# A Fourier-mixing and cosine-gated MLP kernel: rows ahead of constants in the opening, other fillers for TensorE, weight sums on the engines, one transfer per turned row

## The chip, the cores and the metric

One core of one Trainium2 chip. The metric is device time in microseconds (us). A median of several executions is given with its lowest and highest value. The engines are called as in the profile: PE (TensorE), PEld (its weight loads), DVE (VectorE), ACT (ScalarE), POOL (GpSimd) and SP (SyncE, which only issues transfers here).

## The reference

```python
# x: [8, 3008, 256], w_in: [256, 2048], w_out: [2048, 256], all float32
X = np.fft.fft(x, axis=1)
X = np.fft.fft(X, axis=2)
h = X.real.reshape(8 * 3008, 256) @ w_in
g = h * np.cos(h)
out = g @ w_out
```

## The kernel before

The kernel is already tuned. It has an opening of about 37 us, then 376 equal steps that keep PE busy to the end.

*Opening.* The rows of `x` are loaded in four tiles, half of them by row loads and half, in reversed order, by gathers on POOL. DVE adds and subtracts them ("folds" of rows) into even tiles `e` and odd tiles `o`, and halves these once more. PE applies the sequence transform, and DVE and ACT spread the result into rings: `Rr` (real part), `Ir` (imaginary part), `Rb` (channel 128). Meanwhile the channel transform is multiplied into `w_in`, a quarter at a time ("weight folds"), giving `Wc` for the real and `Ws` for the imaginary part:

```python
def fold_sin(q, tag="H"):                  # fold_cos: the same into Wc
    ps = fold_mms(q, 128, tag)
    act(Ws[:, q * 512 : (q + 1) * 512], ps)

def turn_last(q):                          # row 127 of Ws turned into a column
    for f in range(4):
        c = q * 512 + f * 128
        pin(nc.gpsimd.dma_start(out=wex[q][:, f : f + 1], in_=Ws[127:128, c : c + 128]))
```

*A step.* ACT fills a PSUM bank with channel 128's share, and both matmul groups of the step accumulate on it. So the first of them cannot start before this ACT operation is done. Quarter `q` of `wex` serves steps `2q` and `2q + 1` of eight.

```python
def ext(i):
    S = steps[i] = Step()
    S.H = bank("H")
    for j in range(2):
        f = 2 * (i % 8) + j
        act(S.H[:, j * TW : (j + 1) * TW], Rb[:, cols(i)], scale=wex[f // 4][:, f % 4 : f % 4 + 1])

def mm_P(i):
    first_mm(i, Wc, Rr, 128)      # the real product
def mm_Q(i):
    first_mm(i, Ws, Ir, 127)      # the imaginary product
```

After the cosine gate come seven block products with `w_out`, built from sums of blocks of `G` (by POOL, `sum_1` to `sum_4`) and sums of blocks of the weights, `WT`. The latter are made once:

```python
def add_block(k, r, c):                    # 384 KB, added by the transfer itself
    pin(nc.gpsimd.dma_start(
        out=WT[k][:, 2:8], in_=wout[r][:, 2:8, c * 128 : c * 128 + 128], accum_op=ALU.add))

def less_block(k):                         # a negation on ACT
    v = w2.rearrange("p (i r c) -> p i r c", r=2, c=ND)
    act(WT[k][:, 2:8], WT[2][:, 2:8] if k else v[:, 2:8, 0, 0:128], scale=-1.0)
```

*Order of the opening* (`...` marks cuts):

```python
for _ in range(8):                         # one-row matmuls
    mm(bank("M"), zero[:, 0:128], zero[:, 0:1].to_broadcast([1, 512]), True)
sin(halfpi2)
...
fold_sin(0); turn_last(0); fold_cos(0)
warm(10)                                   # ten more of the same
...
fold_now("c0 e0 o0 c3 e3 o3 c2 e2 o2")
add_O(2, 3)
...
halve_now(0, VE[1])
fold_sin(1); turn_last(1)
first_R.early("pA", "pB")
first_R.copy_e()
...
fold_cos(1)
fold_now("o1 O0 I0")
...
halve_now(1, VO[1])
```

Everything that follows is scheduled by a list of pairs of time and operation, in which `T` is the length of a step and `t = 0` the first real product.

Of the kernel before, what the change touches and what calls it, by code (L numbers as in the profile page):

```python
# [118 lines left out]
def kernel(  # L119
# [47 lines left out]
    xflat = x.rearrange("b s d -> (b s) d")  # L167
    ix = cpool.tile([NP, 9], U32, tag="ix")
    nc.sync.dma_start(out=ix, in_=IX_dr.ap())
    L = [cpool.tile([128, NS * ND], FP, tag=f"xl{j}", name=f"xl{j}") for j in range(4)]  # L170

    def gather_x(b, j, a, z, n):

        pin(
            nc.gpsimd.indirect_dma_start(
                out=L[j][0:NP, a * ND : z * ND],
                out_offset=None,
                in_=xflat,
                in_offset=bass.IndirectOffsetOnAxis(ap=ix[:, n : n + 1], axis=0),
                element_offset=b * SEQ * ND,  # L180
            )
        )
# [26 lines left out]
    for g in gathers(0, ORDER):  # L209
        gather_x(*g)  # L210

    CC = cpool.tile([128, 512], FP, tag="CC")
    w1, MC = [], []
# [6 lines left out]
    wout = moe_w_out.rearrange("(i r p) c -> r p i c", r=2, p=128)  # L220
# [24 lines left out]
    load_mats(0)  # L245
    load_w1(1)
    load_mats(1)
    load_w1(2)
    load_w2(0, 4)
    spin(out=WT[2][:, 2:8], in_=wout[0][:, 2:8, 128:256])  # L250
    load_w2(4, NF)
# [18 lines left out]
    nc.gpsimd.memset(R4, 0.0)  # L270
    nc.gpsimd.memset(Rx4, 0.0)
    zero = cpool.tile([1, 264], BF, tag="zero")
    nc.gpsimd.memset(zero, 0.0)
# [46 lines left out]
    def fold_sin(q, tag="H"):  # L320
        ps = fold_mms(q, 128, tag)
        act(Ws[:, q * 512 : (q + 1) * 512], ps)

    def turn_last(q):

        for f in range(4):
            c = q * 512 + f * 128
            pin(nc.gpsimd.dma_start(out=wex[q][:, f : f + 1], in_=Ws[127:128, c : c + 128]))

    def fold_cos(q, tag="H"):  # L330
        ps = fold_mms(q, 0, tag)
        act(Wc[:, q * 512 : (q + 1) * 512], ps)


    def sum_weights(i, k):
# [4 lines left out]
        gtt(  # L340
# [7 lines left out]

    def add_block(k, r, c):

        pin(
            nc.gpsimd.dma_start(
                out=WT[k][:, 2:8], in_=wout[r][:, 2:8, c * 128 : c * 128 + 128], accum_op=ALU.add
            )
        )

    def less_block(k):

        v = w2.rearrange("p (i r c) -> p i r c", r=2, c=ND)
        act(WT[k][:, 2:8], WT[2][:, 2:8] if k else v[:, 2:8, 0, 0:128], scale=-1.0)  # L360
# [17 lines left out]
    def fold_ops():  # L378
# [20 lines left out]
        for key, V, o, a, b, op in (  # L399
            ("E0", VE, 0, 0, 1, ADD),  # L400
            ("E2", VE, 2, 2, 3, ADD),
            ("R0", VE, 1, 0, 2, ADD),
            ("R1", VE, 3, 0, 2, SUB),
            ("O0", VO, 0, 0, 1, ADD),
            ("I0", VO, 1, 0, 2, SUB),
# [67 lines left out]
    def fold_first():  # L473
# [5 lines left out]
        vtt(a, c[0], c[1], ADD)  # L479
        vtt(g, c[2], c[3], ADD)  # L480
        vtt(a, a, g, ADD)
        z = g[:, 0:4]
        run_now(halve(a, z, 0))
# [52 lines left out]
    class Dft:  # L536
# [18 lines left out]

        def copy_e(self):
# [38 lines left out]

        def minus_sum(self):
# [5 lines left out]
            if self.ri == 0:  # L602
                outs.append((R4[:, self.b : self.b + 1], slice(0, 1)))
# [37 lines left out]
    def load_ext():  # L641
        x1 = spool.tile([128, HALF + 1], FP, tag="rx", bufs=1, name="x1")
        rows = [x1[0 : 2 * NB], x1[2 * NB : 4 * NB]]
        state["rows"] = x1[0 : 4 * NB]

# [420 lines left out]
    for _ in range(8):  # L1066
        mm(bank("M"), zero[:, 0:128], zero[:, 0:1].to_broadcast([1, 512]), True)
    sin(halfpi2)
    def warm(n):

        w = bank("M")
        for _ in range(n):
            mm(w, zero[:, 0:128], zero[:, 0:1].to_broadcast([1, 512]), True)

    fold_sin(0)
    turn_last(0)
    fold_cos(0)
    warm(10)
# [15 lines left out]
    first_R, first_I = Dft(0, 0, 0, held(0, (E[1], Z[0]))), Dft(1, 0, 0)  # L1094

    fold_now("c0 e0 o0 c3 e3 o3 c2 e2 o2")
    add_O(2, 3)
    fold_now("E2")
    pin(nc.vector.tensor_copy(out=L[1][0:1, 7 * ND :], in_=L[0][0:1, 0:ND]))
    fold_now("c1 e1 E0 R0")  # L1100
    halve_now(0, VE[1])
    fold_sin(1)
    turn_last(1)
    first_R.early("pA", "pB")
    first_R.copy_e()
    first_x = Dft(0, 0, 0, fold_first(), Rb, True)
    first_x.early("pC", "pD")
    first_x.copy_e()
    fold_cos(1)
    fold_now("o1 O0 I0")  # L1110
    add_O(2, 0)
    first_R.plus()
    first_x.plus()
    halve_now(1, VO[1])
# [74 lines left out]
    def dve_room(n):  # L1189

        step, late = divmod(n, 2)
        if step < 9:
            return 0.64
# [75 lines left out]
    def plan_dft(b, ri, kodd, n):  # L1269

        d = Dft(ri, b, kodd)
# [20 lines left out]
    for t, fn in (  # L1292
        (0.88, lambda: first_I.early("pA", "M")),
        (0.89, first_I.copy_e),
        (0.95, lambda: fold_sin(2, "pC")),
        (0.96, lambda: turn_last(2)),
        (1.0, first_I.plus),
        (2.9, lambda: fold_cos(2, "pA")),
        (T + 0.95, lambda: fold_sin(3, "pC")),
        (T + 2.9, lambda: fold_cos(3, "pA")),  # L1300
        (3 * T, lambda: turn_last(3)),
        (-0.3, lambda: add_block(2, 1, 1)),
        (1.3, lambda: less_block(0)),
        (1.31, lambda: add_block(0, 0, 1)),
        (T + 0.2, lambda: less_block(1)),
        (T + 0.25, lambda: add_block(1, 0, 0)),
    ):
        at(t, fn)
    for k in range(4):
        at(0.1, lambda k=k: sum_weights(0, k))  # L1310
# [3 lines left out]
    p = pool_all(0, FOLD["R1"])  # L1314
    for i in (1, 2, 3):
# [155 lines left out]
```

## Time and profile before

| | before |
|---|---|
| time at the outset, 3 runs | 1939.3 us (1935.9 to 1940.06) |
| span of the profiled execution | 1936.3 us |
| first real product / first imaginary product | 36.90 / 45.84 us |
| first matmul of step 2 / step 4 / step 8 / step 20 | 55.38 / 67.91 / 90.35 / 161.07 us |
| PE idle, first product to 84 us / 84 to 165 / 165 to 1900 | 5.74 / 5.19 / 3.09 us |
| PE at half clock | until 21.3, and 38.3 to 45.1 us |

A step costs 4.75 us of PE and there is nearly no idle time from 165 us on. So the start of step 8 is the best single number of this case: what the opening has won or lost by then should simply be carried to the end. The prediction shows the lines of the profile.

### The profile page before, as it was taken

How to read it: one execution, taken by the hardware profiler on the slowest of the kernel's cores; microseconds unless marked ns; L12 is line 12 of the kernel's file. 1: busy time of each engine (PE TensorE's matmuls, PEld its weight loads, DVE VectorE, ACT ScalarE, POOL GpSimd, SP SyncE). 2: the span in 40 equal slices, each digit the busy share in tenths (PEclk: the TensorE clock that was granted, in tenths of full speed). 3: DMA queues.
4: the chain of work that ended last, by engine and by line, in shares of the span. 5: the costliest groups of instructions: out<-in, count | busy, mean ns of one | idle time of the engine just before them, and what ended most of it. 6: DMA issues, size and time to landing. Idle time of an engine off the chain costs nothing.

```text
span 1936.3 us, 28827 instructions
## 1 busy us (share of the span) xinstructions
PE 1899.4 (98%) x8951; PEld 1646.7 (85%) x8951; DVE 1450.9 (75%) x2366; ACT 1513.3 (78%) x2985; POOL 1525.5 (79%) x2054
## 2 busy tenths in 40 slices
PE   6899999999999999999999999999999999999998
PEld 3778888888888888888888888888888888888887
DVE  5788877777777777777777777777777777777777
ACT  2767888787878887888788887888878887877886
POOL 4879888898888888888889898888878676655654
PEclk9999999999999999999999999999999999999999
DMA  9724211322123112311231113311212110100101
GB/s 216 51 53 85 50 37 24 72 36 51 29 36 69 35 37 49 52 39 32 45 70 29 45 22 61 52 40 30 31 30 36 20 18 17 20 12 12 23 9 25
DMA packets 263490, 82.16 MB, mean 42 GB/s; under 512 B 240841, under 2 KB 246776, under 8 KB 263336
## 3 DMA queue, kind: packets, MB, share of 16 engines
q1 hardware_dynamic: 249240, 49.04, 14.7%
q0 software_dynamic: 11920, 31.01, 9.3%
q8 instruction: 71, 1.16, 0.3%
q14 instruction: 83, 0.68, 0.1%
q10 hardware_dynamic: 2176, 0.26, 0.1%
HBM read 38.29 MB, written 24.69 MB: 33 GB/s over the span
## 4 chain that ended last, share of the span: by engine, by line
PE 87%; ACT 5%; DVE 5%; issue 1%; POOL 1%; DMA 0%; DVEq 0%; POOLq 0%; ACTq 0%
PE H L292 34%; PE pC L292 15%; PE pD L292 15%; PE pB L292 15%; PE pA L292 8%; ACT G L304 1%; DVE G L829 1%; DVE G L298 1%; ACT M L304 1%; ACT E L304 1%; ACT z L304 1%; POOL G L301 1%; ACT H L304 0%; DVE v L298 0%; DVE M L298 0%
## 5 line engine op out<-in xcount | busy, mean ns | idle before, releaser
L301 POOL TENSOR_TENSOR G<-G 128x256 f32<-128x256 f32 x1500 | 1083.7, 734 | 349.7 <-DVE G L829 281.2
L829 DVE SCALAR_TENSOR_TENSOR G<-H,G 128x512 f32<-128x512 f32 x376 | 259.0, 689 | 225.8 <-ACT G L304 223.5
L298 DVE TENSOR_TENSOR G<-H,G 128x512 f32<-128x512 f32 x376 | 259.7, 691 | 216.5 <-ACT G L304 213.3
L292 PE MATMUL H<-Ir,Ws 127*128 127x256 f32 x1504 | 387.8, 379 | 3.8 <-ACT E L304 3.8
L292 PE MATMUL H<-Rr,Wc 128*128 128x256 f32 x1504 | 388.3, 380 | 2.8 <-ACT H L304 2.7
L292 PE MATMUL pC<-G,WT 128*128 128x256 f32 x1504 | 387.0, 379 | 0.7 <-DVE u L298 0.7
L304 ACT ACTIVATE H<-Rb,wex 128x256 f32<-128x256 f32 x752 | 360.0, 479 | 21.9 <-DVE G L829 9.6
L304 ACT ACTIVATE G<-H 128x512 int32<-128x512 f32 x376 | 223.7, 595 | 177.2 <-DVE G L298 177.2
L304 ACT ACTIVATE E<-H 128x512 f32<-128x512 f32 x376 | 223.7, 595 | 167.7 <-PE H L292 166.3
L292 PEld LDWEIGHTS H<-Ir,Ws 127*128 127x128 f32 x1504 | 283.5, 189 | 48.8 <-ACT E L304 8.5
L292 PEld LDWEIGHTS pC<-G,WT 128*128 128x128 f32 x1504 | 284.1, 189 | 43.2 <-PE H L292 1.5
L292 PEld LDWEIGHTS H<-Rr,Wc 128*128 128x128 f32 x1504 | 281.2, 190 | 43.6 <-ACT H L304 5.6
L304 ACT ACTIVATE G<-G,halfpi 128x512 f32<-128x512 f32 x376 | 269.2, 716 | 3.2 <-DVE G L298 3.0
L298 DVE TENSOR_TENSOR G<-E,H 128x512 f32<-128x512 f32 x376 | 255.1, 679 | 4.4 <-ACT Ws L304 2.5
L298 DVE TENSOR_TENSOR M<-G,M 128x512 f32<-128x512 f32 x376 | 257.5, 685 | 0.0
L829 DVE SCALAR_TENSOR_TENSOR G<-G,M 128x512 f32<-128x512 f32 x376 | 254.3, 676 | 0.5 <-ACT M L304 0.5
L304 ACT ACTIVATE M<-M,halfpi 128x512 f32<-128x512 f32 x376 | 245.2, 652 | 0.0
L292 PE MATMUL pB<-G,WT 128*128 128x256 f32 x752 | 225.4, 381 | 4.7 <-POOL G L301 4.7
L304 ACT ACTIVATE M<-G 128x512 int32<-128x512 f32 x376 | 224.1, 596 | 0.0
L292 PE MATMUL pD<-G,w 128*128 128x256 f32 x752 | 223.8, 379 | 0.1
L292 PE MATMUL pA<-G,w 128*128 128x256 f32 x752 | 223.8, 379 | 0.0
L292 PE MATMUL pB<-G,w 128*128 128x256 f32 x752 | 223.7, 379 | 0.0
(157 smaller groups left out, 2054.6 us busy)
## 6 DMA issues: line engine op xcount, KB each, us to landing
out_dram<-ot SPq DMA_DIRECT2D x496, 32.0 KB
xl<-in_x_dram SPq DMA_DIRECT2D x64, 192.0 KB
o<-o POOLq DMA_DIRECT2D x23, 381.0 KB, 4.9
e<-e POOLq DMA_DIRECT2D x21, 384.0 KB, 5.1
out_dram<-ot SPq DMA_DIRECT2D x256, 2.0 KB
Rb<-r SPq DMA_DIRECT2D x10, 376.0 KB
w<-in_moe_w_in_dram SPq DMA_DIRECT2D x4, 512.0 KB
out_dram<-ot SPq DMA_DIRECT2D x64, 28.0 KB
```

The lines of the kernel that those rows point to most:

```text
L292: nc.tensor.matmul(out_, lhsT=lhsT, rhs=rhs, start=start, stop=stop, skip_group_check=True)
L298: pin(nc.vector.tensor_tensor(out=o, in0=a, in1=b, op=op))
L301: pin(nc.gpsimd.tensor_tensor(out=o, in0=a, in1=b, op=op))
L304: pin(nc.scalar.activation(out=o, in_=i, func=func, **kw))
L829: nc.vector.scalar_tensor_tensor(out=o, in0=h, scalar=TWO_PI, in1=c, op0=ALU.mult, op1=ALU.mult)
```

## The change

Its intent is to have the loop begin sooner and with fewer waits, in five parts.

1. *Rows first.* The constants queue behind the rows on SP. A memset of one element of `CC`, which POOL reaches only after its gathers, holds the constants back.
2. *TensorE's fillers.* 60 and then 6 matmuls on 128 rows of ones take the place of 8 and 10 matmuls on one row, to keep the clock up.
3. *Weight sums on engines.* No accumulating transfers and no negations: POOL sums three of the four pairs of blocks, DVE the fourth.
4. *Channel 128's column.* ACT copies the last row of a quarter in another order, and one transfer turns it, in place of four.
5. *Order.* DVE does the real part whole before it begins the imaginary one, small operations leave it for ACT and POOL, and the weight folds of quarters 1 to 3 all stand behind the first real product.

The diff, cut to its core:

```diff
+    ones = spool.tile([128, 512], FP, tag="v", bufs=1, name="ones").bitcast(BF)
+    pin(nc.vector.memset(ones, 1.0))
...
     for g in gathers(0, ORDER):
-        gather_x(*g)
+        gather_x(*g, table=None if g[1] else first_ix)
     CC = cpool.tile([128, 512], FP, tag="CC")
+    pin(nc.gpsimd.memset(CC[0:1, 0:1], 0.0))
...
+    def take_last(q):
+        t = spool.tile([128, 512], FP, tag=("u", "p3")[q % 2], bufs=1, name="wl")
+        act(
+            t[96:128].rearrange("a (p f) -> a f p", f=4),
+            Ws[96:128, q * 512 : (q + 1) * 512].rearrange("a (f p) -> a f p", f=4),
+        )
+        turned[q] = t
     def turn_last(q):
-        for f in range(4):
-            c = q * 512 + f * 128
-            pin(nc.gpsimd.dma_start(out=wex[q][:, f : f + 1], in_=Ws[127:128, c : c + 128]))
+            pin(nc.gpsimd.dma_start(out=wex[q], in_=turned[q][127:128, :]))
...
-    def add_block(k, r, c): ...
-    def less_block(k): ...
...
         for _ in range(n):
-            mm(w, zero[:, 0:128], zero[:, 0:1].to_broadcast([1, 512]), True)
+            mm(w, ones[:, 0:128], ones[:, 128:640], True)
+    warm(60)
...
-    fold_now("c0 e0 o0 c3 e3 o3 c2 e2 o2")
...
+    fold_now("e0 o0 e3 o3 e2 E2 S0 e1 R0")
+    halve_now(0, VE[3])
...
+    warm(6)
+    fold_now("o2 O2 o1 O0 J0")
     add_O(2, 0)
-    halve_now(1, VO[1])
+    halve_now(1, VO[3])
+    first_R.plus_copy()
...
-        (0.96, lambda: turn_last(2)),
...
+        (0.5, lambda: fold_mm(1, 1)),
+        (0.95, lambda: fold_copy(1, 1)),
+        (0.955, lambda: take_last(1)),
+        (0.96, lambda: turn_last(1)),
...
     for k in range(4):
-        at(0.1, lambda k=k: sum_weights(0, k))
+        at(-0.1, lambda k=k: sum_weights(0, k))
     at(-1.5 * T, load_ext)
...
+    for k in range(4):
+        at(0.98, lambda k=k: sum_weights(1, k))
+        on_pool(1, 0.73, lambda k=k: sum_weights(2, k))
```

`load_ext`, which is not itself changed but for one memset, loads channel 128 of `x` as a row, one float of 4 bytes at a time.

## The prediction

> **What bounds the kernel now.** I read the busy shares of the whole page first, then stretches by time, then the opening instruction by instruction.
>
> ```profile
> PE 1899.4 (98%) x8951; PEld 1646.7 (85%) x8951; DVE 1450.9 (75%) x2366; ACT 1513.3 (78%) x2985; POOL 1525.5 (79%) x2054
> PE 87%; ACT 5%; DVE 5%; issue 1%; POOL 1%; DMA 0%; DVEq 0%; POOLq 0%; ACTq 0%
> ```
>
> The first line is the busy line, the second the chain that ended last. TensorE (PE) sets the time. The next table is the stretches view (stretch, its length, busy time of PE, PEld, DVE, ACT, POOL, granted clock, DMA share, GB/s):
>
> ```profile
> 0.00:10.00 10.00, 4.66 (x8) 0.72 (x8) 0.09 (x2) 1.58 (x2) 6.54 (x17) 1.00 0.80 205
> 10.00:20.00 10.00, 1.73 (x2) 0.84 (x3) 6.38 (x9) 0.00 (x0) 1.84 (x2) 1.00 1.04 273
> ...
> 34.90:38.30 3.40, 1.56 (x6) 0.68 (x4) 3.30 (x4) 1.44 (x3) 3.32 (x4) 1.00 1.57 95
> 38.30:45.20 6.90, 6.43 (x19) 5.39 (x20) 1.37 (x3) 0.97 (x2) 1.63 (x3) 0.51 1.95 95
> 45.20:60.00 14.80, 11.17 (x36) 6.33 (x35) 8.83 (x15) 11.63 (x22) 12.74 (x14) 1.00 1.90 37
> ...
> 165.00:1900.00 1735.00, 1731.91 (x8214) 1517.27 (x8213) 1302.89 (x2126) 1402.24 (x2773) 1393.02 (x1871) 1.00 0.20 37
> ```
>
> From 165 us on PE idles 3 of 1735 us, so nothing but the opening can give time here. In the opening PE waits, and from 38.3 to 45.2 us it works at half clock (0.51). The timeline shows what it waits for:
>
> ```profile
> 11.76 1.21 DVE L373 TENSOR_TENSOR e<-xl 96x1016 f32<-96x1016 f32 x1
> ...
> 26.79 1.60 DVE L373 TENSOR_TENSOR e<-e 96x512 f32<-96x512 f32 x3
> ...
> 33.78 0.54 DVE L298 TENSOR_TENSOR Rr<-ab,pB 128x377 f32<-128x377 f32 x1
> ...
> 35.40 3.26 DVE L373 TENSOR_TENSOR o<-o 96x508 f32<-96x508 f32 x3
> ...
> 36.90 1.13 PE L292 MATMUL H<-Rr,Wc 128*128 128x256 f32 x4 [1.57 <-ACT H L304]
> 38.77 1.14 PE L292 MATMUL pA<-MC,o 95*128 95x95 f32 x4 [0.74 <-issue]
> ...
> 43.11 2.90 PE L292 MATMUL pC<-w,CC 128*128 128x512 f32 x4
> ...
> 45.84 1.03 PE L292 MATMUL H<-Ir,Ws 127*128 127x256 f32 x4
> ...
> 59.47 0.70 PE L292 MATMUL pB<-G,WT 128*128 128x256 f32 x2 [2.11 <-POOL G L301]
> ...
> 71.08 0.70 PE L292 MATMUL pB<-G,WT 128*128 128x256 f32 x2 [1.28 <-POOL G L301]
> ```
>
> The real-part fold runs on DVE from 11.7 to 28.4 us, the imaginary one to 38.7. The main loop's first matmul starts at 36.90; its second half (the Ir product) only at 45.84, behind the transform and a weight fold at half clock. Later PE waits for POOL's block sums (2.11 and 1.28 us). The PE gaps between 36.9 and 84 us add up to 5.7 us.
>
> **What the Trainium skill says.** (1) "TensorE: Matmul & The Clock Gate", Part 1: the clock is halved by default and after an idle window of about 3.4 us, and freed after a busy window of that length. The trace agrees: the stretch 34.9 to 38.3 has PE busy only 1.56 us of 3.4, and the next 6.9 us run at 0.51. It also shows what the page does not say: eight matmuls of one row, busy 4.66 us in the first 10, did not free the clock, because the weight loads of the first fold are 0.85 us apart at 19.25, 20.11 and 20.96 and 0.43 apart from 21.54 on. (2) "DMA: Bandwidth & Descriptors", "Issuing engines are not separate DMA queues": all queues share 16 engines and interleave. The trace agrees: 205 to 273 GB/s in total while rows, gathers and constants are under way together. (3) "VectorE: DVE Perf Modes", the errata section: an fp32 two-input operation takes (N+151)/0.96 ns, 1.216 us at N=1016; the trace has 1.21. (4) "GPSIMD Engine Reference", 2.1: a first call after a library load costs about 6 us. Here the first POOL sum took 1.83 us against 0.80 for the next, so I take 1 us for moving that load ahead of the gathers.
>
> **The change, part by part.**
>
> *Rows first.* A memset that POOL can only reach after its eight gathers holds back the constants, queued behind it on SP. Rows and gathers are 8 x 192 KB plus the same again, 3.1 MB. Before, about 1.5 MB of constants took part of the bandwidth and the last gather landed near 19 us. But the gathers are issued one per 1.22 us from 2.58 us, and a table made on POOL (iota) for the first two saves little, since the library load of about 1 us eats it. By bytes at 260 GB/s the first row tile is complete near 11 us (11.7 now), the others near 12, 13.6 and 15.2. So DVE starts 0.7 us sooner, but then never waits.
>
> *DVE's order.* Column copies go to ACT, the channel-128 fold (seven small operations) to POOL, and o2 and o3 are put after the real part. Up to the halving: five folds of 1.13 us spacing (e0 o0 e3 o3 e2), two sums of 1.25, e1 1.13, R0 1.25, halving 2.33 = 12.9, so 23.9 us against 28.4. Then o2, O2, o1, O0, J0 (2 x 1.13 + 3 x 1.24 = 6.0) and halving 2.3: 32.2 against 38.7. The first Rr copy stands behind this on DVE: 32.7.
>
> *TensorE before the loop.* 60 full-height matmuls at some 0.22 us (0.43 cold) fill 1.3 to about 16 us, so the first fold (constants in near 17 us) runs warm: 3.4 us. It isn't on the path, which is DVE's. First main matmul: 32.7, 4.2 us sooner.
>
> *From there on the PE order.* Before, from the first main matmul (step 0) to that of step 8: 36.90 to 90.35, 53.5 us. Its work: eight P and Q pairs of 1.73 (13.8), six X groups of 3.03 (18.2), transform parts 1.73 + 2.45, four folds of 1.73 (6.9): 43.1. The rest is gaps 5.7, half clock 3.4 (half of 6.9), 1.3 of small latencies. After, two more folds stand behind that point (quarters 1 to 3 of both weights): 43.1 + 3.5 + 1.3 = 47.9 without gaps. That puts step 8 at 32.7 + 47.9 = 80.6 against 90.35: 9.8 us sooner at best.
>
> *Block sums.* Three accumulating DMAs of 384 KB and two ACT negations of 0.83 us go. POOL gets eleven and DVE four sums of 0.73. Between 30 and 60 us POOL then has about 9 us of sums of weights, 3 of transfers and 12 of the loop's sums: 24 of 30. The folds spread through the first four steps give it time, since PE needs about 6.5 us for such a step.
>
> *Channel 128's column.* 16 transfers of 0.56 us of POOL time each become four of about 1 us, plus four ACT copies of 0.5. It frees POOL 5 us; ACT has about 19 us of work in the 21 us of steps 0 to 3, its tightest stretch.
>
> **The rivals.** *The clock is halved again.* My PE work before the loop ends near 29 us, 6 filler matmuls included, and the first main matmul comes at 32.7: 3.8 us idle. Before, a 3.4 us stretch with 1.56 us busy was enough for the throttle. If it comes, up to 6.9 us at half clock, 3.4 us lost. Against it: the fillers are placed for this, and the window's phase can be kind. I give it one half: 1.7 us. *A new bound in steps 0 to 4.* ACT's order is strict, and ACT and POOL are nearly full; the gaps of 5.7 us would then come back in part. Hand-placing every ACT, DVE and POOL operation of four steps I found no PE wait, but the trace shows DVE operations stretched beside POOL (the sum at 69.8 us waited for one), so I take 2 us. All gaps back would leave 4 us of gain. *Nothing, because the loop absorbs it.* If a later transfer or the second batch set the pace, the gain would vanish; but PE has 3 us of gaps after 165 us, and a shift of PE passes to the end. That leaves small chances in 84 to 165 us, where some 5 us of gaps stand now. *Slower:* an unforeseen wait for a constant, say w1 of quarters 2 and 3 now last; by bytes they land near 36 us and are needed at 42.
>
> **Range and chances.** 9.8 less 1.7 less 2, about 6.5 to 7 us, with a little for the second rival: 1939.3 - 7 = 1932 us, 0.4% less. With no stall 1929; with throttle and all gaps 1936. Repeats of before spread over 4 us. The range is 1927 to 1937. Two per cent would be 39 us, as long as the whole opening, so within 2% it is almost surely: 0.98; faster 0.01, slower 0.01.
>
> **What would show it.** Right: first row tile's fold on DVE near 11 us, real halving done near 24 and imaginary near 32; first main matmul near 32.7, the Ir product near 38.5 (45.84), step 4 near 60 (67.91), full clock between 30 and 50; and from 165 us on the same trace, some 7 to 9 us earlier. Wrong: DVE waiting for rows (then gathers, not DVE, bound the opening); a granted clock of 0.5 after 32 us; PE waits on ACT or POOL of over 3 us in steps 0 to 6; or the shift present at step 8 and gone by step 20.

## The result, and the profile after

| | runs | median (lowest to highest) | ratio to before, 95% |
|---|---|---|---|
| before | 4 | 1937.6 us (1934.77 to 1940.06) | |
| after | 4 | 1935.72 us (1933.57 to 1937.39) | 0.999 (0.997 to 1.0011) |

A ratio is the mean time of one kernel's fast runs over that of the other's in the same rounds, so it is not quite the ratio of the medians beside it. The change is within 2%, and its interval of four runs each holds 1. A second set of runs of the same kernel, below, gave 0.9989. All outputs are right.

The stretches view of the changed kernel (stretch, its length, busy time of PE, PEld, DVE, ACT and POOL with counts, granted clock, DMA share, GB/s):

```profile
0.00:10.00 10.00, 7.99 (x25) 3.12 (x26) 1.35 (x4) 1.80 (x3) 7.12 (x13) 1.00 0.79 218
10.00:20.00 10.00, 8.01 (x38) 3.54 (x36) 9.37 (x9) 1.07 (x4) 5.59 (x14) 1.00 0.96 248
...
31.40:34.80 3.40, 1.30 (x5) 1.06 (x6) 2.88 (x6) 0.96 (x3) 2.68 (x4) 1.00 1.09 317
34.80:38.20 3.40, 3.40 (x8) 1.72 (x7) 0.00 (x0) 0.92 (x2) 0.00 (x0) 0.50 1.50 112
...
165.00:1900.00 1735.00, 1731.91 (x8212) 1518.08 (x8211) 1302.86 (x2125) 1402.56 (x2772) 1393.40 (x1869) 1.00 0.20 37
```

The last line is the loop: PE is busy for 1731.91 us, to the hundredth what it was before. DVE's 9.37 us in the second line, against 6.38, say that it hardly waits for rows any more (0.39 us ahead of the second tile). The stretches at half clock in these traces last 3.41 us or a multiple of it; one such length is called a window here, and work at full clock is called warm. The fourth line is one window at half clock, after a window in which PE was busy for only 1.30 us. Before, two such windows stood there. Another half-clock window of the changed kernel, from 21.1 to 24.6 us, fell on its first weight folds.

The timeline of the changed kernel answers to the one in the prediction (start, length, engine and line, operation, tiles, shape, count, and in brackets the idle time just before with what ended it):

```profile
9.57 1.21 DVE L375 TENSOR_TENSOR e<-xl 96x1016 f32<-96x1016 f32 x1 [7.61 <-DMA xl<-in_x_dram,ix]
...
21.56 1.59 DVE L375 TENSOR_TENSOR e<-e 96x512 f32<-96x512 f32 x3
...
29.91 2.98 DVE L375 TENSOR_TENSOR o<-o 96x508 f32<-96x508 f32 x3
...
32.81 0.54 DVE L609 COPY Rr<-pA 128x377 f32<-128x377 f32 x1
...
33.49 1.10 PE L298 MATMUL H<-Rr,Wc 128*128 128x256 f32 x4 [2.15 <-DVE Rr L609]
...
40.88 1.13 PE L298 MATMUL H<-Ir,Ws 127*128 127x256 f32 x4 [0.71 <-DVE Ir L304]
46.74 1.13 PE L298 MATMUL H<-Ir,Ws 127*128 127x256 f32 x4 [0.43 <-ACT E L310]
```

The first real product stands 3.4 us sooner (33.49 for 36.90), the first imaginary one 5.0 us (40.88 for 45.84), and no wait for POOL's block sums is left. Steps 4, 8 and 20 begin at 63.59, 85.75 and 155.83 us: 4.3, 4.6 and 5.2 us sooner. The span ends 4.6 us sooner (1931.7 for 1936.3). This profiled execution, 1933.57 us, is the fastest of the four. On the mean the gain is some 2 us, which these runs do not tell from none.

That the end simply follows step 8 can be checked on every kernel, since each left a trace. Span less the start of step 8 was 1845.95 us before and 1845.95 us after. In the twelve traces of the experiments it lies between 1845.77 and 1846.09, but for two in which a half-clock window fell in the loop, at 117 and 111 us (1846.54 for "column of `x` later", 1846.85 for "five moves together"). So, but for this, each difference told below arises ahead of step 8, and where a time is told beside a milestone, the milestone explains it.

### The profile page after: what moved, and what is told of

Read it like the earlier page. It is cut to its first block, busy times and chain, and to the rows that moved or that the text cites. A ratio compares the mean times of both kernels' runs of the same rounds, so it can differ in the third digit from the quotient of the medians.

```text
span 1931.7 us, 28919 instructions
## 1 busy us (share of the span) xinstructions
PE 1908.5 (99%) x9000; PEld 1652.0 (86%) x9000; DVE 1456.5 (75%) x2367; ACT 1519.5 (79%) x2993; POOL 1521.4 (79%) x2044
## 4 chain that ended last, share of the span: by engine, by line
PE 87%; DVE 5%; ACT 5%; issue 1%; POOL 1%; DMA 0%; SPq 0%; DVEq 0%; POOLq 0%
PE H L298 34%; PE pC L298 15%; PE pD L298 15%; PE pB L298 15%; PE pA L298 7%; ACT G L310 1%; DVE G L845 1%; DVE G L304 1%; ACT E L310 1%; ACT M L310 1%; ACT z L310 1%; DVE v L304 1%; ACT H L310 0%; DVE M L304 0%; DVE o L375 0%
## 5 line engine op out<-in xcount | busy, mean ns | idle before, releaser
L298 PEld LDWEIGHTS pC<-G,WT 128*128 128x128 f32 x1504 | 285.1, 190 | 43.1 <-PE H L298 1.5
```

The costliest lines, as they stand in the source:

```text
L298: nc.tensor.matmul(out_, lhsT=lhsT, rhs=rhs, start=start, stop=stop, skip_group_check=True)
```

## The experiments

The prediction's theory: DVE sets the first product, and the rest of the gain is lost to half clock and to waits in the first steps that come and go. A second theory, formed on the traces: the new order makes one wait of its own, which has a name and can be taken away. A third: some part of the change costs time by itself, and undoing it makes the kernel faster. The expectations quoted below number their theories as they stood then. Twelve kernels ran, four to a job, each job on one chip with eleven runs of the kernel before (medians 1938.27, 1937.89 and 1938.62 us). The edits are against the changed kernel unless it is said otherwise.

| variant | runs | median (lowest to highest), us | ratio to before, 95% | first product | step 2 | step 8 |
|---|---|---|---|---|---|---|
| the same again | 5 | 1935.29 (1934.21 to 1938.28) | 0.9989 (0.9976 to 1.0002) | 34.16 | 51.57 | 87.56 |
| more fillers | 5 | 1935.34 (1934.47 to 1937.29) | 0.9988 (0.9975 to 1.0001) | 33.51 | 50.73 | 87.64 |
| copy ahead of the halving | 5 | 1932.61 (1931.85 to 1933.1) | 0.997 (0.9957 to 0.9983) | 33.70 | 49.17 | 85.18 |
| one-row fillers | 6 | 1940.46 (1936.89 to 1941.91) | 1.0008 (0.9995 to 1.002) | 39.71 | 56.58 | 92.58 |
| column of `x` later | 5 | 1933.95 (1931.46 to 1934.36) | 0.9976 (0.9963 to 0.9989) | 33.69 | 50.16 | 85.26 |
| constants not held | 6 | 1939.07 (1934.44 to 1941.21) | 1.0005 (0.9992 to 1.0017) | 37.09 | 51.62 | 86.83 |
| four transfers | 5 | 1933.67 (1930.7 to 1934.13) | 0.9977 (0.9964 to 0.999) | 33.65 | 48.02 | 83.12 |
| no fillers | 6 | 1935.55 (1931.85 to 1939.58) | 0.9987 (0.9973 to 1.0) | 33.38 | 53.25 | 90.93 |
| sums by transfer | 6 | 1931.8 (1930.5 to 1936.1) | 0.9977 (0.9963 to 0.999) | 32.30 | 47.75 | 82.64 |
| before, with fillers | 6 | 1937.03 (1934.8 to 1939.21) | 0.9995 (0.9983 to 1.0007) | 41.41 | 55.80 | 90.81 |
| five moves together | 5 | 1927.52 (1926.69 to 1928.07) | 0.9945 (0.9932 to 0.9958) | 30.75 | 44.25 | 79.35 |
| these, four transfers | 5 | 1928.8 (1926.73 to 1929.48) | 0.9952 (0.9939 to 0.9965) | 30.11 | 43.89 | 79.48 |

The milestones are those of the one profiled execution, which need not be the median one: that of "constants not held" is near its fastest (1934.74 us), that of "no fillers" near its slowest (1938.62 us), and those of "four transfers" (1930.7 us) and "sums by transfer" (1930.5 us) are the fastest of their sets.

### The same kernel again

No edit. It tells how much two executions of one kernel differ, and where.

> The changed kernel as it is, once more. Its four times so far lie in two groups, 1933.6 and 1934.2 against 1937.3 and 1937.4, and those of the kernel before as well, 1934.8 and 1935.9 against 1939.3 and 1940.1. Theory C (the clock's window): the two groups are one or two more half-clock windows of 3.41 us in the opening, and which an execution gets depends on how the free-running window lies; then there are again groups some 1.7 or 3.4 us apart, and the mean gain is 2 to 5 us. Theory N (noise of transfers): times spread evenly, with no relation to the half-clock records. The profile shows where the half-clock stretches lie: in the changed kernel's first profile at 21.1 to 24.6 and 34.8 to 38.2 us.

The wait comes and goes, as the prediction's theory has it. But the trace gives it a name. The timeline of this second execution:

```profile
39.04 0.58 POOL L348 DMA_DIRECT2D wex<-wl  x1 [4.21 <-ACT wl L310]
...
45.36 0.60 ACT L310 ACTIVATE Ws<-H 128x512 f32<-128x512 f32 x1
50.53 0.99 ACT L310 ACTIVATE H<-Rb,wex 128x256 f32<-128x256 f32 x2 [4.57 <-DMA wex<-wl]
51.57 1.13 PE L298 MATMUL H<-Rr,Wc 128*128 128x256 f32 x4 [3.26 <-ACT H L310]
```

Read from the bottom: the first matmul of step 2 waits 3.26 us for ACT's `H`, and that ACT operation had waited 4.57 us for a transfer, the turned row of the second quarter (the code's quarter 1, which serves steps 2 and 3). POOL issued it at 39.04, and it landed 11.4 us later. It carries 2 KB. In the first execution the same row was issued at 39.7 and landed at 48.6, just in time (0.14 us of PE idle). In the kernel before its four parts were issued from 28.5, the last had landed at 35.4 (most of the 4-byte packets follow from 35.5 on), and they were needed at 53. The tile view of the kernel before, for the six such transfers between 24 and 36 us:

```profile
DMA to landing us min/median/max: 4.9/5.2/5.4
```

So the change has moved this small transfer from well ahead of its use to just before it. This speaks for the second theory.

The two executions of the one kernel also lose different things. The first had a half-clock window and 2.69 us of PE idle between the first product and 84 us; the second had full clock there and 5.51 us idle.

### More fillers

```diff
-    warm(60)
+    warm(70)
...
-    warm(6)
+    warm(22)
```

> The changed kernel with more filler matmuls: 70 for 60 at the start, 22 for 6 ahead of the first main matmul, so that TensorE is not idle from 17.8 to 19.8 and from 31.4 to 33.5 us. Theory C: no half-clock stretch after about 7.5 us; the first folds end some 1.7 us earlier (not on the path), the work from 34.8 to 38.2 us runs at full clock, so the Ir product starts 1.7 us sooner (about 39.2 for 40.9), the time is 1.5 to 2 us under the changed kernel's better group, and the spread of five runs falls under 1.5 us. Rival (the idle gaps are not what throttles): half-clock stretches stay, and time and spread are those of the changed kernel. Rival 2: the extra fillers get in the way and the first main matmul starts later than 33.5.

The second filler group ran to 33.3 us and the clock was full from 7.3 to 51.7 us. The imaginary product came at 39.24 us, 1.6 us sooner than in the first execution. All of that went into the wait at step 2 (3.07 us; the row landed 11.2 us after its issue), and then a half-clock window from 51.7 to 55.1 followed that wait. The mean time did not move (0.9988 against 0.9989). So the half clock ahead of the loop, which the prediction had as the first rival, is not what holds this kernel back while the wait at step 2 stands behind it.

### The copy of Rr ahead of the imaginary halving

```diff
-    warm(60)
+    warm(70)
...
-    halve_now(1, VO[3])
     first_R.plus_copy()
+    halve_now(1, VO[3])
```

> The changed kernel with 70 fillers at the start and the first copy of Rr moved ahead of the imaginary halving on DVE. If DVE's order is what holds the first main matmul (it waited 2.15 us for that copy), it starts near 31 to 32 us for 33.5, and the first weight fold behind it fills the time until the imaginary part is ready; the Ir product comes at 37 to 38 for 40.9, and the whole is 3 to 5 us faster than the changed kernel. If instead the landing of channel 128's column (31.2) or the imaginary halving (32.9) sets the pace, the gain is 1 to 2 us, and if the copy on DVE only moves the wait to the imaginary part, it is that of the fillers alone, 1.7.

Ratio 0.997, with runs within 1.3 us of each other. The first product did not come sooner (33.70): with the copy out of the way it waited for ACT's `H` (2.97 us) in place of DVE's `Rr`. The timeline shows what ACT had waited for:

```profile
32.66 0.99 ACT L310 ACTIVATE H<-Rb,wex 128x256 f32<-128x256 f32 x2 [3.79 <-DMA wex<-wl]
33.70 2.07 PE L298 MATMUL H<-Rr,Wc 128*128 128x256 f32 x4 [2.97 <-ACT H L310]
```

It is the turned row of the first quarter, issued at 25.91 and landed 6.7 us later. So close behind DVE's chain stands a second bound on the first product, the landing of that row. The second quarter's row landed at 48.0 and the wait at step 2 stayed away, with 2.29 us of PE idle to 84, although one window (33.3 to 36.7 us) was at half clock. The interval lies below 1, but overlaps the changed kernel's own (0.9976 to 1.0002). Yet all five runs (1933.1 at most) lie below all five of the same kernel again in the same job (1934.21 at least), so a gain is likely. Where it comes from, and why these runs lie so close together, is open.

### Fillers of one row

```diff
-            mm(w, ones[:, 0:128], ones[:, 128:640], True)
+            mm(w, zero[:, 0:128], zero[:, 0:1].to_broadcast([1, 512]), True)
```

> The changed kernel with its fillers (60 and 6) made of one row, as those of the kernel before, instead of 128 rows. If only full-height matmuls count as activity, the clock stays halved until the first folds at 19.8 us have filled a window, about 25 us, and falls again after the idle stretch near 32: half clock from about 35 for two windows instead of one, so 1.7 to 3.4 us slower than the changed kernel. The fillers themselves, 60 of 0.43 us, would end at 27.6 and hold the first fold until then, which can put 1 us or more on top. If height doesn't matter, the trace has full clock from 7.5 us on as in the changed kernel, and the time is the same.

The timeline, and under it the stretches view of this variant:

```profile
1.11 25.78 PE L298 MATMUL M<-zero 1*128 1x512 bf16 x60 [1.11 <-POOL zero L171]
26.82 6.69 PE L298 MATMUL H<-w,CC 128*128 128x512 f32 x8
...
38.48 0.55 DVE L609 COPY Rr<-pA 128x377 f32<-128x377 f32 x1 [6.97 <-PE pA L298]
```

```profile
2.00:25.00 23.00, 23.00 (x56) 7.90 (x55) 14.61 (x15) 2.98 (x9) 14.62 (x23) 1.00 0.97 271
```

PE is busy for all of 23 us and still each filler takes 0.43 us (25.78 / 60), twice the 0.22 us that the full-height ones reach warm, so they end at 26.9 us, and the weight folds behind them run cold too (6.69 us, against 5.37 in the changed kernel, part of which was cold too). A word on the clock column: it says 1.00 up to 32.9 us here, yet the lengths of the matmuls show half speed, so where the column has no record of a throttle the lengths decide. By the lengths the clock is freed at 32.9 us. Here PE, not DVE, sets the first product: the copy of `Rr` on DVE sat idle for 6.97 us until PE's `pA`. It comes at 39.71, and the mean is some 3.7 us above the changed kernel's, with intervals that just overlap. So these fillers did not free the clock and the full-height ones did. Height is not the only difference: they multiply zeros and not ones, and no run parts the two. On the means, 66 one-row matmuls look worse than none (1.0008 against 0.9987 for "no fillers"), but these intervals overlap too.

### The column of x later

```diff
         (0.96, lambda: turn_last(1)),
+        (0.965, load_ext),
...
-    at(-1.5 * T, load_ext)
```

> The changed kernel, with the loads of x's channel 128 (some 25,000 packets of 4 bytes, from 32 to 70 us) released only after the transfer of the second quarter of channel 128's weights is issued (near 40 us), not before it (31 us). In two of the profiles that transfer landed 10 to 11 us after its issue and TensorE stood 3.1 to 3.3 us at 48 us; in the first profile it landed some 8 us after and cost 0.1. Theory W (the small packets in the way): the transfer lands within 5 us, the wait at step 2 (near 48 us) is under 0.2 us, the spread of five runs drops below the 4 us of the changed kernel, and the mean is 1 to 2.5 us lower. Rival Q (the transfer is slow by itself, 128 pieces of 16 bytes): the landing stays 8 to 11 us and the wait as often. Rival L: the loads now end 8 us later and hold the column's own fold near 88 us, giving it back.

This is the test of the second theory. The loads of `x`'s channel 128 (two of 48 KB, some 25,000 packets of 4 bytes, most of them between 35 and 62 us in the first execution) are issued behind the turned row instead of ahead of it. The tile view and the timeline of this variant:

```profile
DMA to landing us min/median/max: 2.0/2.0/2.0
```

```profile
41.06 0.58 POOL L348 DMA_DIRECT2D wex<-wl  x1 [7.39 <-ACT wl L310]
41.63 0.76 POOL L660 MEMSET x<- 32x768 f32 x1
...
47.87 0.98 ACT L310 ACTIVATE H<-Rb,wex 128x256 f32<-128x256 f32 x2
50.16 1.03 PE L298 MATMUL H<-Rr,Wc 128*128 128x256 f32 x4
```

The same view of the second execution of the changed kernel:

```profile
DMA to landing us min/median/max: 11.4/11.4/11.4
```

Nothing but the place of these loads (and of the one memset that goes with them) differs, and the landing falls from 11.4 to 2.0 us. ACT's operation has no wait before it any more (no bracket), and step 2 follows on without one. The wait is thus shown to come from these loads. The row now lands at 43.1, before the bulk of the 4-byte packets begins (44.5), and isn't needed before 47.87. The delay beside them is not one number: in the nine traces of variants of the changed kernel with the loads issued ahead of the row, the changed kernel's two among them, the second quarter's row took 6.8 to 12.2 us. The ratio is 0.9976, with less PE idle to 84 (1.99 us). Step 8 stands no sooner than in the first execution, since this one was at half clock for two windows (31.9 to 38.7 us). From 0.9989, taken on another chip, that is 2.5 us less, where the wait at step 2 of the two executions above was 0.14 and 3.26 us; the two intervals overlap, so the size of the gain is not settled.

### The constants not held back

```diff
-    pin(nc.gpsimd.memset(CC[0:1, 0:1], 0.0))
```

> The changed kernel without the memset that holds the constants behind the gathers. Theory (rows first sets DVE's start): the first fold on DVE starts near 11.5 us for 9.57, DVE waits between tiles, the real halving ends near 26 for 23.1, and the first main matmul is 2 to 3 us later than 33.5; the constants land sooner, so the first weight fold starts by 18 us. The time is 2 to 3 us over the changed kernel. Rival (DVE's order alone made the gain, the rows come early enough in any case): within 0.5 us at the first main matmul.

The first row tile still arrives early (DVE starts at 9.92 us; 9.57 with the hold), but the others come later, and DVE's first folds of the four tiles start at 9.92, 13.26, 16.36 and 20.08 us for 9.57, 12.30, 14.56 and 18.27. The real halving starts at 22.64 for 20.84, the imaginary one at 30.99 for 29.19. So what the hold buys in this trace is 1.8 us of DVE. The profiled execution also ran its transforms at half clock, from 24.7 to 38.3 us, so its first product stands 3.6 us later, at 37.09. The ratio of 1.0005 has nothing left of the change's gain, but its interval overlaps the changed kernel's, so the loss is not shown on the time. What the hold and what the clock do to it was not parted.

### Four transfers for a row

```diff
     def take_last(q):
-        t = spool.tile(...)
-        act(t[96:128]..., Ws[96:128, ...]...)
-        turned[q] = t
+        pass
     def turn_last(q):
-            pin(nc.gpsimd.dma_start(out=wex[q], in_=turned[q][127:128, :]))
+        for f in range(4):
+            c = q * 512 + f * 128
+            pin(nc.gpsimd.dma_start(out=wex[q][:, f : f + 1], in_=Ws[127:128, c : c + 128]))
```

> The changed kernel with four column transfers per quarter as before, and without the four ACT copies (1.1 us each) that turn the row. If one transfer per quarter helps by freeing POOL: POOL spends 1.7 us more per quarter, and the sums wait, 0.5 to 2 us slower. If the ACT copies cost more than they give: the waits of TensorE on ACT in steps 0 to 3 (0.8 us in all) go, the transfers start 1.1 us sooner, and the time is the same or up to 1.5 us lower. 512 pieces of 4 bytes per quarter beside the small packets could also land later: then the wait at step 2 grows to 3 us or more every time.

Undoing this part shows no cost: 0.9977. No copy of 1.1 us on ACT stands before a row's issue here, and the wait at step 2 stayed away in the profiled execution. That execution also escaped the throttle, and it is worth a look why, in the stretches view:

```profile
28.25:31.67 3.42, 1.55 (x8) 0.52 (x6) 3.32 (x4) 0.95 (x2) 2.08 (x3) 1.00 1.08 382
31.67:35.08 3.41, 1.43 (x6) 1.12 (x7) 2.77 (x6) 0.29 (x1) 2.56 (x4) 1.00 1.14 281
```

PE idled 3.85 us in a row here, more than the 2.15 us ahead of the first product in the changed kernel. But the idle time fell across two windows, with 1.55 and 1.43 us of work in them, and neither throttled. In the changed kernel a window with 1.30 us throttled. In the kernel before, one with 1.56 us did. So a window's busy time alone, at this resolution, doesn't decide; the exact rule stays open.

### No fillers

```diff
-    warm(60)
...
-    warm(6)
```

> The changed kernel without its fillers, 60 and 6. The one-row version lost 5 us, but its 60 slow fillers held the first folds until 26 us, so it doesn't tell what full height is worth. Without fillers the first folds start at 17 to 18 us at half clock, 6.9 us long, to about 25; full clock from 25 or later; half clock again after the idle stretch near 31. If the clock alone is what fillers give, the work from the first main matmul on costs 1.7 to 3.4 us more than in the changed kernel: 1937 to 1939. If the fillers are not needed, since the first folds are not on the path: within 1 us of 1935.3.

The mean is the changed kernel's (0.9987), with a spread of 7.7 us. The first product comes at 33.38, against 33.49 with fillers, and waits 3.17 us for DVE's `Rr`. So here the first product isn't set by PE's early work, fillers or not, but by DVE, as the prediction said. There is more half clock: it held until 24.2, from 34.4 to 37.8, and from 51.5 to 58.3 us, against until 7.5, from 21.1 to 24.6 and from 34.8 to 38.2 us in the changed kernel. The means show no gain from the fillers. The last stretch follows the wait at step 2, in the timeline:

```profile
53.25 2.08 PE L298 MATMUL H<-Rr,Wc 128*128 128x256 f32 x4 [4.05 <-ACT H L310]
```

PE idles for more than a window here, and the four matmuls that follow take 2.08 us where four take 1.03 to 1.13 warm.

### The weight sums by transfer

```diff
+    spin(out=WT[2][:, 2:8], in_=wout[0][:, 2:8, 128:256])
...
+    def add_block(k, r, c): ...            # as in the kernel before
+    def less_block(k): ...
+        (-0.3, lambda: add_block(2, 1, 1)),
+        (1.3, lambda: less_block(0)),
+        (1.31, lambda: add_block(0, 0, 1)),
+        (T + 0.2, lambda: less_block(1)),
+        (T + 0.25, lambda: add_block(1, 0, 0)),
...
-        at(0.98, lambda k=k: sum_weights(1, k))
-        on_pool(1, 0.73, lambda k=k: sum_weights(2, k))
+        if k:
+            on_pool(3, 0.73, lambda k=k: sum_weights(k, 3))
...
-        n = on_dve(max(n, 11), 0.35, lambda k=k: sum_weights(3, k, vtt))
```

> The changed kernel with block weights 1 to 7 summed as before: one more load of 384 KB, three accumulating transfers, two negations of 0.83 us on ACT, three sums on POOL. If summing on the engines matters: ACT has 1.7 us more in the tight steps 0 and 1, POOL is held by transfers of 1 to 3 us and TensorE waits for POOL's sums again (1 to 3 us near 55 to 70 us), 1 to 3 us slower. If not (POOL has slack, since the folds stretch the first steps): within 1 us, as TensorE in the changed kernel never waits on POOL in the first 84 us; the second quarter's column, now behind two more accumulating transfers, could then land later and bring the 3 us wait of step 2 each time.

Undoing part 3 shows no cost either: 0.9977 (0.9963 to 0.999). The imaginary halving takes 2.71 us on DVE in place of 3.70, the first product stands at 32.30, and the row of the second quarter is issued at 37.2 and lands at 43.9, 1.5 us ahead of its use. The intervals overlap with the changed kernel's, so "faster" isn't shown. That the sums on the engines give time in this order of things isn't seen either; PE's waits for POOL's sums, which the expectation named as a danger, did not come.

### The kernel before, with fillers only

```diff
+    ones = spool.tile([128, 512], FP, tag="v", bufs=1, name="ones").bitcast(BF)
+    pin(nc.vector.memset(ones, 1.0))
...
-            mm(w, zero[:, 0:128], zero[:, 0:1].to_broadcast([1, 512]), True)
+            mm(w, ones[:, 0:128], ones[:, 128:640], True)
+    warm(64)
...
     fold_cos(1)
+    warm(6)
     fold_now("o1 O0 I0")
```

> The kernel before with full-height fillers alone: 64 for its 8 of one row at the start, 10 of full height for its 10 of one row, and 6 more in the idle time ahead of the first main matmul. If the fillers are worth something by themselves: full clock from about 7.5 us, no half-clock stretch at 38 to 45 us, so the transform and the fold there take 3.4 us less, the Ir product starts at 42.4 for 45.8, and the time is 2 to 3.4 us under the kernel before, with the spread of its runs (5 us) smaller. If the waits for POOL at 57 and 70 us swallow it, the time is within 1 us of before.

This edit is against the kernel before; it does one part of the change alone. Ratio 0.9995: nothing. The profiled execution was throttled sooner than that of the kernel before, in the stretches view:

```profile
25.50:28.90 3.40, 1.40 (x6) 0.57 (x5) 3.19 (x9) 0.60 (x1) 1.45 (x3) 1.00 1.16 295
28.90:39.20 10.30, 10.30 (x34) 8.88 (x34) 6.69 (x11) 2.22 (x4) 6.23 (x8) 0.50 1.23 245
```

A window with 1.40 us of work, and then three windows at half clock although PE was busy all through the 10.30 us: with transforms of 94 and 95 rows from 28.5 to 36.8, and with a full-height weight fold from there, 2.4 us into which the clock was freed. The first product came at 41.41, 4.5 us later than before. Still step 8 stands at 90.81 against 90.35: the half clock that the kernel before has from 38.3 to 45.1 us, during the imaginary transform, did not come. In this execution the fillers moved the half clock; they didn't take it away.

### Five moves together

The moves that the runs above speak for, and two that follow from them.

```diff
-    warm(60)
+    warm(70)
...
-    first_x = Dft(0, 0, 0, fold_first(), Rb, True)
-    add_E(0, 1)
     fold_copy(0, 1)
     take_last(0)
+    first_stat = fold_first()
+    first_x = Dft(0, 0, 0, first_stat, Rb, True)
     turn_last(0)
+    add_E(0, 1)
...
-    warm(6)
-    fold_now("o2 O2 o1 O0 J0")
+    fold_mm(1, 1)
+    warm(2)
+    fold_now("o2 O2 o1 O0")
+    first_R.plus_copy()
+    fold_now("J0")
     add_O(2, 0)
     halve_now(1, VO[3])
-    first_R.plus_copy()
...
-        (0.5, lambda: fold_mm(1, 1)),
-        (0.95, lambda: fold_copy(1, 1)),
-        (0.955, lambda: take_last(1)),
-        (0.96, lambda: turn_last(1)),
+        (-0.25, lambda: fold_copy(1, 1)),
+        (-0.2, lambda: take_last(1)),
+        (-0.15, lambda: turn_last(1)),
+        (-0.12, load_ext),
...
-        (2.3, lambda: fold_mm(1, 0, "pD")),
-        (T + 0.87, lambda: fold_copy(1, 0)),
+        (0.5, lambda: fold_mm(1, 0, "pD")),
+        (0.98, lambda: fold_copy(1, 0)),
...
-    at(-1.5 * T, load_ext)
```

That is: the first turned row goes ahead of the accumulating transfer of 384 KB; the copy of `Rr` goes ahead of `J0` and the halving; a weight fold that the loop needs anyway takes the place of fillers in PE's idle time before the first product; the second turned row can therefore go before the loop; and the 4-byte loads follow it. The run also begins with 70 fillers, puts the real part's transform ahead of channel 128's (cut here), and draws the second quarter's other weight fold forward.

> A version drawn from the runs so far: 70 fillers at the start; the turned row of the first quarter sent ahead of the accumulating transfer; the first copy of Rr on DVE before the last imaginary sum and halving; the second quarter's sine fold in the idle time ahead of the first main matmul, in place of fillers, with its row sent at once; channel 128's loads after that. Expected: first main matmul at 30 to 31 us (33.5), the Ir product at 36 (40.9), step 4 at 57 to 58 (63.6 to 65.4), no wait of over 1 us at step 2, and 1927 to 1930 us, 5 to 8 under the changed kernel. If the loop's first steps are bound by ACT and POOL rather than by when they start, the gain stays under 3 us.

The timeline:

```profile
27.77 0.55 DVE L609 COPY Rr<-pA 128x377 f32<-128x377 f32 x1 [0.18 <-PE pA L298]
28.59 1.88 PE L298 MATMUL H<-w,CC 128*128 128x512 f32 x4
30.19 1.59 DVE L375 TENSOR_TENSOR o<-o 96x508 f32<-96x508 f32 x3
30.75 1.13 PE L298 MATMUL H<-Rr,Wc 128*128 128x256 f32 x4
36.48 1.13 PE L298 MATMUL H<-Ir,Ws 127*128 127x256 f32 x4 [0.71 <-DVE Ir L304]
41.57 1.13 PE L298 MATMUL H<-Ir,Ws 127*128 127x256 f32 x4 [1.37 <-ACT E L310]
44.25 1.03 PE L298 MATMUL H<-Rr,Wc 128*128 128x256 f32 x4
```

The copy of `Rr` stands 5.0 us sooner, the fold runs where fillers ran, the first product comes at 30.75 without a wait in front of it (no bracket), and the halving's three operations take 1.59 us in place of 2.98; POOL isn't summing beside them here. The second row was issued at 32.7, landed at 39.5 and was needed at 41.9: 6.8 us, although the 4-byte loads were issued behind it. Their packets begin at 36 us here, and until then constants and an accumulating transfer were under way, so going ahead of these loads does not by itself make a row land in 2.0 us. Step 8 stands 6.4 us sooner than in the first execution of the changed kernel and 11.0 sooner than before. The ratio is 0.9945 (0.9932 to 0.9958): some 10.7 us less than before, and its interval lies clear of the changed kernel's own. It beats both kernels. Which of its moves gives how much was not parted, but its first product has won 2.7 us of the 6.4 and what follows up to step 8 the rest; 1.73 us of that is the fold that now stands ahead.

### These five moves with four transfers for a row

```diff
     def take_last(q):
+        pass
     def turn_last(q):
+        for f in range(4): ...             # as in "four transfers"
```

> The version drawn from the runs, with four column transfers per quarter and no ACT copies to turn the row. TensorE's wait on ACT at 40 us (1.37 us) should shrink by about 1.1, the copy's length, and the transfers start 1.1 us sooner; POOL has 1.7 us more per quarter. If ACT is the bound of the first steps: 1926 to 1927 for 1927.5. If POOL's time or the 4-byte pieces matter: 1928 to 1930.

0.9952 against 0.9945, intervals overlapping nearly whole: one transfer or four for a row makes no difference that these runs can show. The two ran on different chips, so the comparison goes by way of the kernel before.

## Why the prediction was right or wrong

The time on record was 1932 us, in a range of 1927 to 1937. Measured were medians of 1935.72 and 1935.29: inside the range, in its upper part, and within 2% as said. The mechanism held in its main line: DVE sets the first product, PE's work from there on is as counted, and the end follows step 8. The two rivals that it made allowance for both came, and with them two of its own four signs of being wrong: a clock of 0.5 after 32 us (34.8 to 38.2) in the first execution, and a wait of PE on ACT of over 3 us in steps 0 to 6 (3.26 us at step 2) in the second. That the time still fell inside the range owes something to luck: the allowance of 2 us for waits was made with busy engines in mind, and a transfer used it up. Point by point, with the first and the second execution:

| term | predicted | first | second |
|---|---|---|---|
| first real product | 32.7 | 33.49 | 34.16 |
| from there to step 8, without gaps and half clock | 47.9 | 47.87 | 47.89 |
| half clock in that stretch | 1.7 | 1.7 | 0 |
| PE idle in that stretch | 2 | 2.69 | 5.51 |
| step 8 | 80.6 at best, 84.3 with both | 85.75 | 87.56 |
| gain at step 8 | 9.8 - 1.7 - 2 = 6.1 | 4.6 | 2.8 |

The second row is worked out: start of step 8 less first product, less half a window of 3.4 us in the first execution, less the idle time (85.75 - 33.49 - 1.7 - 2.69 = 47.87; 87.56 - 34.16 - 5.51 = 47.89). So the count of PE work fits these two executions. It isn't as close everywhere: the same sum for "four transfers" is 0.8 us off.

**The main term that was mis-sized.** "Channel 128's column" was priced in issue time and ACT's copies alone, and no wait was put down for it. The prediction did name "a new bound in steps 0 to 4" in which ACT's strict order matters, took 2 us, and added that hand-placing found no PE wait. That placing names the operations of ACT, DVE and POOL, and no landing of a transfer. With the second quarter's fold moved behind the first real product, its row is issued after the 4-byte loads have begun. It took 8.9 and 11.4 us to land in the two executions (6.8 to 12.2 in nine traces), where each transfer of that quarter took about 5 in the kernel before, and 2.0 with those loads behind it. It was in time in one execution (0.14 us) and not in the other (3.26 us). "Column of `x` later" shows the cause.

**DVE's chain.** "23.9 us" for the real halving's end was 23.15 (21.56 + 1.59): DVE had its first rows at 9.57, not near 11. "32.2" for the imaginary one was 32.89, since the halving took 3.70 us in place of 2.3. POOL's first weight sums run in just that stretch (30.71 to 34.2 us), and in the runs where they do not (one-row fillers, five moves) the halving takes 2.31. It was the prediction that had warned of DVE operations stretched beside POOL, but at a later place. The copy of `Rr` followed at 32.81, as predicted (32.7), and the product 0.7 us behind it. That this agrees is luck in part: rows 1.4 us early and a halving 1.4 us long cancel. And the chain was not the only bound: with the copy moved ahead of the halving the first product still came at 33.70, since the first quarter's row landed at 32.6, which the prediction had not counted.

**The clock.** The throttle was given one half, at a cost of 1.7 for the mean; it came in one of the two executions, as one window, which cost 1.7. "Full clock between 30 and 50" was wrong for the first and right for the second. PE was idle for 2.15 us ahead of the first product, not 3.8. That one-row matmuls do not free the clock was read off weight loads at 19.25 us, before which PE had been idle for 11.98 us; those loads cannot show it, and the run with one-row fillers does. That the half clock settles little is shown by "more fillers": full clock there, and no time won.

**Smaller terms.** Copies of the turned row take 1.1 us on ACT, not 0.5. The wait before the first gather is 0.47 us, not 1. The first filler group ends at 17.83 us, not 16, and the first weight fold starts at 19.82, not 17, with 2.00 us of waiting for `w`. It did not run warm in 3.4 us: it took 5.37 us, with a half-clock window on it. Neither was on the path, as predicted. The imaginary product came at 40.88 and 39.89, not 38.5, and step 4 at 63.59 and 65.41, not 60. POOL makes twelve sums of weights in the code, not eleven. "Small chances in 84 to 165 us" was right: idle there is 4.56 us, for 5.19.

**Rounding and baseline.** The prediction's own sum is 6.1 us, and it was written as "6.5 to 7". Its worst case, "1936 with throttle and all gaps", does not follow from its terms either: 9.8 less 3.4 less 5.7 leaves 0.7 us of gain, or 1938.6 us, above the range; the slowest runs of the two sets took 1937.39 and 1938.28 us. The gain was also taken from a baseline of 1939.3, a median of three runs, where eleven runs each gave 1938.27, 1937.89 and 1938.62. Of the some 3.5 us between 1932 and what was measured, about 1 is the baseline and 0.9 the rounding. The rest is in the table.

**What stays open.** Times of one kernel spread over 1.3 to 7.7 us. Both the windows of the clock and the landing of the row differ between executions, and each explains several us in the traces at hand. But only one execution of each set of runs has a trace, so which of them makes the spread cannot be told.

## What to carry to other kernels

Before pricing a reordering, list for each small transfer when it is issued, what shares the queues with it then, and when its result is needed: a transfer of 2 KB that had 17 us to spare became a wait of up to 3.26 us in a change that was to gain 6. In a kernel whose loop has no idle time, one milestone at the loop's start predicts the end to 0.2 us here, but for two traces of fourteen with half clock in the loop (0.6 and 0.9 us), so variants can be compared by it. And where an engine must be kept busy ahead of the loop, fill it with work that the loop needs anyway, as the weight fold in "five moves together", rather than with work that is thrown away.

## What the Trainium skill lacked or had wrong

- *"TensorE: Matmul & The Clock Gate", Part 1.* This part names one busy window of about 3.4 us as enough to free the clock. One-row matmuls, on zeros, did not do it: PE was busy 23.00 of 23.00 us between 2 and 25 us in the run with 60 of them, each still took 0.43 us, and the clock was freed at 32.9. Nor did transforms of 94 and 95 rows in the kernel before with fillers: 8.3 us of them without a break (28.5 to 36.8 us) passed, from 28.9 us on at half clock (0.50), which ended at 39.2, in the full-height fold behind them.
- *The same section* has the clock halved after an idle window. Windows that were partly busy came just before half clock too: 1.30, 1.40 and 1.56 us busy of 3.4. Two with 1.43 and 1.55 did not. The page gives no threshold, and these runs don't find one.
- *"DMA: Bandwidth & Descriptors", "Queues, rings and completion order" and "Rules for kernel authors".* The page says that each DMA engine alternates between queues by packets, and that a strided last dimension makes one descriptor per element. The trace agrees with the second (some 25,000 packets of 4 bytes for two loads of 48 KB, most of them from 35 to 62 us). What is missing is what that costs another transfer: 2 KB took 6.8 to 12.2 us to land beside them in nine traces, and 2.0 us in the one where the queues were empty ahead of them.
- *"GPSIMD Engine Reference", 2.1,* names about 6 us for a first call after a library load. In the changed kernel the first gather waited 0.47 us, and the longest of POOL's first sums in the opening took 1.17 us; no wait of that size shows. Whether a load of the library fell inside the profiled span, the trace does not tell.
